# A gated pair of 2-D spectral filters: another layout for the narrow column's inverse and the scratch reads, merged constants, another order list

## The chip, the cores and the metric

The kernel runs on one core of a Trainium2 chip. The metric is the device time of one execution in microseconds (us); lower is better. Five engines work side by side, each on its own in-order queue: TensorE (PE; its weight loads are shown as PEld), VectorE (DVE), ScalarE (ACT), GpSimd (POOL) and SyncE (SP). Here SyncE issues nearly all DMA transfers, and sixteen DMA engines carry them.

## The reference

Two spectral filters, A and B, act on the same input `x` (1 x 2048 x 1024, bf16), and a gate per row mixes their results. `B_x` is not used.

```python
def filt(x, w_r, w_i):                          # w: 2048 x 513
    X = jnp.fft.rfft2(x.astype(jnp.float32), axes=(-2, -1))
    return jnp.fft.irfft2(X * (w_r + 1j * w_i), s=(2048, 1024),
                          axes=(-2, -1)).astype(jnp.bfloat16)

x = A_x
g = sigmoid((x * gate_w).sum(-1, keepdims=True))
out = g * filt(x, A_w_r, A_w_i) + (1 - g) * filt(x, B_w_r, B_w_i)
```

## The kernel before

All transforms are matmuls with constant matrices. The 2048 rows are split as `s = 16 * s2 + s1`, with `s2` on the 128 partitions and `s1` along the free dimension. The 1024 columns are folded by symmetry into sums and differences, so that the frequencies fall into an odd half (`par` 1) and an even half (`par` 0), each 256 wide. The frequency 512 of the column transform is left over: it is the "narrow column", handled by small steps of its own.

**Forward.** `ld x` loads the rows in nine transfers; `fold` (L228, VectorE) makes sums and differences; `f1` (L236, or `f1u`, L243, which does without a fold) transforms over `s2`; `ye` copies PSUM to the tile `y`. Then come eight units `u` (0 to 3 odd, 4 to 7 even). For each: `f2` (column transform, constant FD), `te` (copy), `f3` (over `s1`, constant WF), `xe` (copy), `prod` (VectorE, products with both filters' weights from a buffer `W`; two of the four buffers lie inside the tile `r`), `i1` (inverse over the 16 row frequencies, constant WI, in two halves), `re` (copy into one of three slots `rl`), and `wr` (L336), which writes the slot to a scratch tensor `scr` in DRAM, in 1 KB pieces.

**Scratch and inverse.** `rd` (L340) reads the scratch back with another meaning of the partitions: each of the 128 partitions gets `n` x 2 KB in one piece for `n` values of `s1`. `rd` of the odd half needs units 0 to 3 in scratch, `rd` of the even half units 4 to 7. It lands in the tile `r`, half `par`. For each pair of `s1` values, `v` from 0 to 7, `i2` (L371) multiplies by the gate's weighted matrices EA and EB, `ve` copies, `i3` or `i3u` (L387, L395, constant IG) does the column inverse, `ce`, `se` or `ue` copy, `pm` or `pmp` make sums and differences, `fin` joins the odd and the even half, and `st` (L434) stores. The odd half's inverse runs first; the even half's follows once `rd 0` has landed.

**Narrow column.** `l1`, `l2` (forward), `lp` (products, L297), `l3` (inverse, six matmuls, L301), `l3e` (copy to `zl`). Then `lx` (L311): a scatter of `zl` to the DRAM scratch `scn` in pieces of 4 bytes, and a load of it into `NL` with the other meaning of the partitions. `lf` (L315) copies parts of `NL` into the even half of `r`, over columns that `rd 0` has brought in, before `i2` reads them.

**Gate.** `gws` and `gh` (L344) transform the gate's weights, `zse` (L351) copies the result to `zs` and at once issues the load of `zt` from it; `gz` (L355), `sig`, and `gw` (L363), which makes EA and EB from the sigmoid `g` and the constant E.

**Order.** One list, `ORDER`, written out by hand at the end of the file, gives every step in turn. Each engine, SyncE too, takes its steps in the order of the list, and dependencies between tiles become semaphore waits. A letter says which engine does a copy or an elementwise step (`a` ScalarE, `d` VectorE, `p` GpSimd). So a transfer on SyncE that waits for its data holds back all transfers behind it. Eight semaphores are shared by the DMA transfers in turn, so that a transfer also waits for the one eight places ahead of it. All copies go through one helper (L196), all matmuls into eight PSUM banks `ps`.

Of the kernel before, what the change touches and what calls it, by code (L numbers as in the profile page):

```python
# [35 lines left out]
def make_constants():  # L36
# [8 lines left out]
    for q in range(64):  # L45
# [10 lines left out]
        E[2 * q], E[2 * q + 1] = ec, es  # L56
# [8 lines left out]
    c["F1"] = _bf16np(np.concatenate([F, -F, F], axis=1))  # L65
    c["EZ"] = _bf16np(EZ.reshape(128, 128) / 128)
    c["E"] = _bf16np(E)
    al = al.reshape(NT, 4 * 32, 32)
    c["WF"] = _bf16np(np.stack([-al.imag, al.real, al.imag], axis=2).transpose(1, 0, 2, 3))
# [9 lines left out]
    c["WI"] = _bf16np(np.tile(z.transpose(2, 0, 1, 3), (4, 1, 1, 1)))  # L79
    z = np.stack([np.concatenate([be.imag, -be.imag], axis=1), np.concatenate([be.real, be.real], axis=1)], axis=1)  # L80
    c["WN"] = _bf16np(np.tile(z.transpose(2, 0, 1, 3), (2, 1, 1, 1)))
# [17 lines left out]
    FN = -np.cos(np.pi * i)  # L99
    c["FD"] = _bf16np(FD.reshape(2, 128, 2, 2, 256).transpose(1, 2, 3, 0, 4))  # L100
    c["FN"] = _bf16np(FN.reshape(2, 128).T)
# [7 lines left out]
def gated_mix(ctx, tc, x_in, w_in, wn_in, gw_in, out, order):  # L109
# [18 lines left out]
    F1 = sb("f1", [3, 128])  # L128
    gws = sb("gws", [8])
    nc.scalar.dma_start(F1[:], dr["F1"].rearrange("p (a b) -> p a b", a=3))  # L130
    nc.scalar.dma_start(gws[:], gw_in)
# [7 lines left out]
    scn = dp.tile([2 * NT, 64, 2], BF16, name="scn")  # L139
    y = sb("y", [2, 2, 2, 64, NS1, 2])  # L140
    FD = sb("fd", [2, 2, 2, 256])
    FN = sb("fn", [2])
    nc.scalar.dma_start(FN[:], dr["FN"])
    WF = sb("wf", [NT, 3, 32])
    WI = sb("wi", [2, 3, 64])
    WN = sb("wn", [2, 2, 32])
    EZ = sb("ez", [128])
# [11 lines left out]
    wl = sb("wl", [2, 2 * NT, 2])  # L159
    pl = sb("pl", [2, 2 * NT, 2])  # L160
    zl = sb("zl", [2 * NT, 2])
    NL = sb("nl", [NS1, 2])
# [40 lines left out]
    def ld(what, *a):  # L203
        if what == "x":
            s0, n = a
            nc.sync.dma_start(x[:, s0:s0 + n, :], xv[:, s0:s0 + n, :])
        elif what == "w":
            u, s = a
            nc.sync.dma_start(flat(W[s]), w_in[u])
        elif what == "wl":  # L210
            nc.sync.dma_start(wl[:], wn_in.rearrange("p (t s a) -> p t s a", t=2, a=2))
        elif what == "wf":
            nc.sync.dma_start(WF[:, a[0]:a[1]], dr["WF"][:, a[0]:a[1]])
        else:
            t_ = {"FD": FD, "WI": WI, "WN": WN, "EZ": EZ, "E": E, "IG": IG}[what]
            nc.sync.dma_start(t_[:], dr[what])

    def gws_(eng):

        nc.vector.tensor_scalar(gh[:], gws[:], 0.25, None, ALU.mult)  # L220
# [76 lines left out]
    def lp(eng):  # L297
        xb = xl[:].rearrange("p (t s a) -> p t s a", t=1, a=1).to_broadcast([P, 2, 2 * NT, 2])
        nc.vector.tensor_tensor(pl[:], xb, wl[:], ALU.mult)

    def l3(g0):  # L301
        v = pl[:].rearrange("p t s a -> p t (s a)")
        for i, (o, lo, hi) in enumerate(((0, 2, 64), (64, 0, 64), (0, 0, 2))):
            for k in range(2):
                nc.tensor.matmul(PS[o // 2:o // 2 + 32, g0, lo:hi], lhsT=WN[o:o + 64, int(i == 2), k, :], rhs=v[o:o + 64, k, lo:hi],
                                 start=(k == 0), stop=(k == 1))

    def l3e(g0, eng):
        copy(eng, zl[0:64].rearrange("p s a -> p (s a)"), PS[0:64, g0, 0:64])

    def lx():  # L311
        nc.sync.dma_start(scn[:].rearrange("s p a -> p s a"), zl[0:64])
        nc.sync.dma_start(NL[:], scn[:].rearrange("s (j x) a -> (s j) x a", x=NS1))

    def lf(s0, n, eng):  # L315
        copy(eng, R[:, 0, s0:s0 + n, 512:1024:256], NL[:, s0:s0 + n, :])
# [23 lines left out]
    def rd(par, s0, n, t0=0, nt=NT):  # L340
        src = scr[par, 2 * t0:2 * t0 + 2 * nt].rearrange("t (j s r) c -> (t j) s (r c)", s=NS1, r=2)
        nc.sync.dma_start(R[8 * t0:8 * t0 + 8 * nt, par, s0:s0 + n, :], src[:, s0:s0 + n, :])
# [8 lines left out]
    def zse(g0, eng="a"):  # L351
        copy(eng, zs[:].rearrange("p q c s -> p (q c s)"), PS[:, g0, :])
        nc.sync.dma_start(zt[:], zs[0:97:32].rearrange("p q c s -> p (q c s)"))

    def gate_z(h, g0):  # L355
        for s in range(8):
            nc.tensor.matmul(PS[:, g0 + s // 4, (s % 4) * 128:(s % 4) * 128 + 128],
                             lhsT=zt[:, 8 * h + s:8 * h + s + 1].to_broadcast([P, 128]), rhs=EZ[:], start=True, stop=True)

# [74 lines left out]
    def st(v, s0=0, n=2):  # L434
# [3 lines left out]
               l3e=l3e, lx=lx, lf=lf, prod=prod, i1=i1, re=re, wr=wr, rd=rd, gws=gws_, gh=gate_hat, zse=zse, gz=gate_z, sig=sig,  # L438
# [73 lines left out]
def pack_w(mats):  # L512
# [4 lines left out]
    for q in range(64):  # L517
        rows = np.concatenate([(kk + 128 * k1) % S for kk in pair_k2(q)])
        v = a[rows].reshape(32, 2, 2, -1)
        for r in range(2):  # L520
            for z in range(2):
                wn[q % 2, r, :, z, q // 2] = v[:, :, (r + z) % 2, 512]
# [44 lines left out]
```

## Time and profile before

| | us |
|---|---|
| median of 3 runs | 129.66 (128.72 to 133.2) |
| profiled execution | 128.86 |
| its span, first to last instruction | 127.0 |

| engine | busy us | share of the span |
|---|---|---|
| VectorE | 98.5 | 77% |
| TensorE matmul | 97.9 | 77% |
| ScalarE | 87.9 | 69% |
| TensorE weight load | 71.6 | 56% |
| GpSimd | 2.6 | 2% |

The profile is of one execution. "Granted clock" is the TensorE clock in parts of full speed; it was 0.938 over the span. The sixteen DMA engines moved 36.34 MB. The page's slices show the span in 40 parts of 3.2 us; the digits are tenths of the time in which the DMA engines were busy, and the line below gives what they moved:

```profile
DMA  3999999991003999899999999999712999409884
GB/s 99 287 362 419 430 410 397 424 400 44 0 5 129 254 427 378 285 341 331 341 379 396 374 295 377 391 356 357 85 13 32 417 428 415 175 31 351 312 323 172
```

The page's issue rows give, for each kind of transfer, its size and the median time from issue to landing:

```profile
r<-scr SPq DMA_DIRECT2D x7, 1024.0 KB, 7.4
w<-in_w_dram SPq DMA_DIRECT2D x6, 1024.0 KB, 10.5
scr<-rl SPq DMA_DIRECT2D x12, 512.0 KB, 6.2
...
out_dram<-p SPq DMA_DIRECT2D x4, 512.0 KB, 2.6
```

Elsewhere a row such as `101.58 0.29 PE L378 MATMUL ... [5.94 <-DMA r<-scr]` has the start in us from the span's start, the length, the engine, the line of the kernel and its operation with output and input; the bracket has the idle time ahead of it and what ended it.

### The profile page before, as it was taken

To read this page: it belongs to the slowest core of one execution; us is meant where nothing else is said; L and a number is where in the kernel's file an instruction comes from. 1 tells how busy PE (TensorE), PEld (TensorE's weight loads), DVE (VectorE), ACT (ScalarE), POOL (GpSimd) and SP (SyncE) were. 2 spreads that over 40 slices of the span, in tenths; PEclk is the share of its full clock that TensorE was granted. 3 is DMA by queue.
4 is the path that set the end of the run, shared out by engine and by line. 5 is a ranking of instruction groups with operands and counts; after the bars stand their busy time and mean duration, and the time that the engine had idled before them with its cause. 6 is when DMAs were issued, how large, how long until landed. Compare 5 with 4: busy or idle time off the path is not lost. (4 is left out here: it accounts for less than half of the span.)

```text
span 127.0 us, 3857 instructions
## 1 busy us (share of the span) xinstructions
PE 97.9 (77%) x1695; PEld 71.6 (56%) x1696; DVE 98.5 (77%) x135; ACT 87.9 (69%) x86; POOL 2.6 (2%) x6
## 2 busy tenths in 40 slices
PE   6849998279897797969695998699991099999900
PEld 2538787156664465447344545278990099998300
DVE  0259898295999999998999577996892048999970
ACT  3139873187999999995986499976660058999630
POOL 1000000000000000000000420000000000000000
PEclk9999999958999999999999589999998559999996
DMA  3999999991003999899999999999712999409884
GB/s 99 287 362 419 430 410 397 424 400 44 0 5 129 254 427 378 285 341 331 341 379 396 374 295 377 391 356 357 85 13 32 417 428 415 175 31 351 312 323 172
DMA packets 17828, 36.34 MB, mean 286 GB/s; under 512 B 3988, under 2 KB 12436, under 8 KB 15892
## 3 DMA queue, kind: packets, MB, share of 16 engines
q1 hardware_dynamic: 17380, 36.00, 78.4%
q8 instruction: 13, 0.21, 0.6%
q10 hardware_dynamic: 432, 0.10, 0.4%
q14 instruction: 3, 0.02, 0.0%
HBM read 23.51 MB, written 12.59 MB: 284 GB/s over the span
## 5 line engine op out<-in xcount | busy, mean ns | idle before, releaser
L320 DVE TENSOR_TENSOR p<-x,w 128x2048 bf16<-128x2048 bf16 (+1 forms) x22 | 28.0, 1315 | 1.5 <-DMA w<-in_w_dram 0.9
L196 ACT CAST rl<-ps 128x1536 bf16<-128x1536 f32 (+2 forms) x16 | 23.2, 1470 | 2.6 <-PE ps L330 2.3
L330 PE MATMUL ps<-p,wi 32*64 32x512 bf16 x512 | 20.0, 409 | 4.3 <-ACT rl L196 1.2
L378 PE MATMUL ps<-g,r 128*128 128x128 bf16 x128 | 16.8, 229 | 5.9 <-DMA r<-scr 5.9
L378 PEld LDWEIGHTS <-r 128*128 128x128 bf16 x256 | 16.3, 103 | 6.8 <-DMA r<-scr 6.1
L196 ACT CAST y<-ps 128x1024 bf16<-128x1024 f32 (+1 forms) x17 | 14.2, 904 | 8.0 <-PE ps L240 7.3
L240 PE MATMUL ps<-f,r 128*128 128x256 bf16 x124 | 15.9, 290 | 3.2 <-DVE r L230 1.8
L378 PE MATMUL ps<-e,r 128*128 128x128 bf16 x128 | 16.8, 229 | 0.0
L240 PEld LDWEIGHTS <-r 128*128 128x128 bf16 x124 | 12.7, 104 | 6.1 <-DVE r L230 2.5
L330 PEld LDWEIGHTS <-wi 32*64 32x64 bf16 x512 | 9.1, 110 | 12.1 <-issue 8.8
L196 ACT CAST x<-ps 128x1024 bf16<-128x1024 f32 (+2 forms) x8 | 11.6, 1446 | 6.0 <-PE ps L271 6.0
L259 PE MATMUL ps<-fd,y 128*128 128x256 bf16 x128 | 15.2, 273 | 0.1
L230 DVE TENSOR_TENSOR r<-r 128x1024 bf16<-128x1024 bf16 (+1 forms) x16 | 10.3, 670 | 6.4 <-DMA r<-in_x_dram 6.3
L196 ACT CAST w<-ps 128x1024 bf16<-128x1024 f32 (+1 forms) x15 | 12.9, 953 | 1.8 <-PE ps L378 1.6
L259 PEld LDWEIGHTS <-y 128*128 128x128 bf16 x128 | 12.0, 98 | 3.3 <-issue 1.1
L196 ACT CAST t<-ps 128x1536 bf16<-128x1536 f32 (+3 forms) x9 | 12.2, 1350 | 1.9 <-PE ps L259 1.7
L196 DVE CAST rl<-ps 128x512 bf16<-128x512 f32 (+1 forms) x11 | 9.6, 879 | 2.3 <-ACT g L361 1.4
L271 PE MATMUL ps<-t,wf 32*32 32x256 bf16 (+1 forms) x384 | 6.5, 308 | 6.1 <-DMA wf<-cst_wf 2.3
L428 DVE TENSOR_TENSOR p<-p,y 128x1024 bf16<-128x1024 bf16 x16 | 10.2, 685 | 0.2
L271 PEld LDWEIGHTS <-wf 32*32 32x32 bf16 x384 | 4.6, 88 | 9.7 <-issue 6.2
L320 DVE TENSOR_TENSOR p<-x,r 128x2048 bf16<-128x2048 bf16 (+1 forms) x6 | 9.3, 1572 | 0.0
L196 DVE CAST w<-ps 128x512 bf16<-128x512 f32 x3 | 2.1, 689 | 7.5 <-PE ps L378 7.2
(55 smaller groups left out, 97.5 us busy)
## 6 DMA issues: line engine op xcount, KB each, us to landing
r<-scr SPq DMA_DIRECT2D x7, 1024.0 KB, 7.4
w<-in_w_dram SPq DMA_DIRECT2D x6, 1024.0 KB, 10.5
scr<-rl SPq DMA_DIRECT2D x12, 512.0 KB, 6.2
r<-in_x_dram SPq DMA_DIRECT2D x7, 512.0 KB, 7.8
r<-in_w_dram SPq DMA_DIRECT2D x2, 1024.0 KB, 11.2
scr<-rl SPq DMA_DIRECT2D x2, 1024.0 KB, 9.1
out_dram<-p SPq DMA_DIRECT2D x4, 512.0 KB, 2.6
out_dram<-p SPq DMA_DIRECT2D x8, 256.0 KB, 2.3
```

Of the source, the lines that this page charges most:

```text
L196: (nc.scalar.copy if eng == "a" else nc.vector.tensor_copy)(out=out, in_=in_)
L230: e.tensor_tensor(xf[uv][:, s0:s0 + n, :], x[:, s0:s0 + n, 0:512], x[:, s0:s0 + n, 512:1024], (ALU.add, ALU.subtract)[uv])
L240: nc.tensor.matmul(PS[:, g0 + k, blk * 256:blk * 256 + 256], lhsT=xf[uv][:, s0 + k, h * 256 + blk * 128:h * 256 + blk * 128 + 128], rhs=fn ...
L259: nc.tensor.matmul(PS[:, g0 + b, 256 * cs:256 * cs + 256], lhsT=y[:, par, blk, KK[par, cs], 4 * t:4 * t + 4].rearrange("p q s c -> p (q s ...
L271: nc.tensor.matmul(PS[qo:qo + 32, g0 + b, dst:dst + ln], lhsT=WF[32 * a:32 * a + 32, t, w, :], rhs=T[0][32 * a:32 * a + 32, b, src:src + l ...
L320: nc.vector.tensor_tensor(pr[u % 2][r][:, b0:b0 + nb], xb, W[s][:, b0:b0 + nb], ALU.mult)
L330: nc.tensor.matmul(PS[o:o + 64, g0 + 2 * (b % 2) + a // 2, :], lhsT=WI[q:q + 32, int(t == 0 and a == 0), ws, :], rhs=rhs, start=(k == 0), ...
L378: nc.tensor.matmul(PS[:, g0 + s, 128 * c:128 * c + 128], lhsT=R[:, par, s1, o:o + 128], rhs=Ew[:, s1, :], start=(ab == 0), stop=(ab == 1))
L428: e.tensor_tensor(OT[v % 4][:, :, k].rearrange("p s e m -> p e s m"), a, b, (ALU.add, ALU.subtract)[k])
```

## The change

Four things change.

The narrow column's inverse. `l3` now takes the products as the stationary operand and the constant WN as the moving one, so that the result leaves TensorE with row pairs on partitions, as `i2` wants them. It has 24 small matmuls instead of six; `l3e` copies straight to `NL`; `lx`, the scratch `scn` and the tile `zl` are gone. The products tile `pl` doubles to 256 elements per partition.

The partitions. For this the 128 partitions of the second half are ordered as (4, 32) and no longer as (32, 4): the constant E is reordered on the host, and `rd` reads `scr` with another pattern. Its source was 128 pieces at one stride; now it is 4 groups of 32 pieces, carried in the instruction as 4, then 32, then 4096 (or 2048) contiguous elements. The destination is the same 128 partitions of `r`.

The loads. F1 and FN come in one load (ScalarE's queue); the gate's weights come with `wl`; WF, WI, WN and EZ become one tile CW of 2176 columns with one load. `zt` is a step of its own (`ztd`), apart from `zse`.

The order list is new throughout. `f1u` is no longer used. `w 1` is loaded ahead of CW, and `w 0` behind it; IG goes behind `wr 0`, `wr 1` and `w 4`; E goes ahead of `wr 0`. `gh` and `zse` come after unit 1, and both halves of `gw` of the second half go to GpSimd. On SyncE the first `rd` stands ahead of `w 7`, and the last odd `rd` behind all `wr`.

```diff
-        E[2 * q], E[2 * q + 1] = ec, es
+        for cc, e in enumerate((ec, es)):
+            E[32 * (2 * (q % 2) + cc) + q // 2] = e
...
+    c["CW"] = np.concatenate([a.reshape(128, -1) for a in (WF, WI, WN, EZ)], axis=1)
...
     def lp(eng):
-        xb = xl[:].rearrange("p (t s a) -> p t s a", t=1, a=1).to_broadcast([P, 2, 2 * NT, 2])
-        nc.vector.tensor_tensor(pl[:], xb, wl[:], ALU.mult)
+        xb = xl[:].rearrange("p (k a t) -> p k a t", k=1, a=1).to_broadcast([P, 4, 2, 2 * NT])
+        nc.vector.tensor_tensor(pl[:], xb, wl, ALU.mult)
...
     def l3(g0):
-        v = pl[:].rearrange("p t s a -> p t (s a)")
-        for i, (o, lo, hi) in enumerate(((0, 2, 64), (64, 0, 64), (0, 0, 2))):
-            for k in range(2):
-                nc.tensor.matmul(PS[o // 2:o // 2 + 32, g0, lo:hi], lhsT=WN[o:o + 64, int(i == 2), k, :], rhs=v[o:o + 64, k, lo:hi],
-                                 start=(k == 0), stop=(k == 1))
+        for j in range(4):
+            o, cc = 64 * (j // 2), j % 2
+            for ab in range(2):
+                for k in range(4 if o == 0 else 2):
+                    nc.tensor.matmul(PS[32 * j:32 * j + 32, g0, 16 * ab:16 * ab + 16], lhsT=pl[o:o + 64, k, ab, :],
+                                     rhs=WN[o:o + 64, k // 2, k % 2, 16 * cc:16 * cc + 16], start=(k == 0), stop=(k == (3 if o == 0 else 1)))
 
     def l3e(g0, eng):
-        copy(eng, zl[0:64].rearrange("p s a -> p (s a)"), PS[0:64, g0, 0:64])
-
-    def lx():
-        nc.sync.dma_start(scn[:].rearrange("s p a -> p s a"), zl[0:64])
-        nc.sync.dma_start(NL[:], scn[:].rearrange("s (j x) a -> (s j) x a", x=NS1))
+        copy(eng, NL[:].rearrange("p a s -> p (a s)"), PS[:, g0, 0:32])
 
     def lf(s0, n, eng):
-        copy(eng, R[:, 0, s0:s0 + n, 512:1024:256], NL[:, s0:s0 + n, :])
+        copy(eng, R[:, 0, s0:s0 + n, 512:1024:256], NL[:, :, s0:s0 + n].rearrange("p a s -> p s a"))
...
-    def rd(par, s0, n, t0=0, nt=NT):
-        src = scr[par, 2 * t0:2 * t0 + 2 * nt].rearrange("t (j s r) c -> (t j) s (r c)", s=NS1, r=2)
-        nc.sync.dma_start(R[8 * t0:8 * t0 + 8 * nt, par, s0:s0 + n, :], src[:, s0:s0 + n, :])
+    def rd(par, s0, n):
+        src = scr[par].rearrange("t (j s) c -> j t (s c)", j=4)
+        nc.sync.dma_start(R[:, par, s0:s0 + n, :], src[:, :, 1024 * s0:1024 * (s0 + n)])
...
+    def ztd():
         nc.sync.dma_start(zt[:], zs[0:97:32].rearrange("p q c s -> p (q c s)"))
```

SyncE's transfers from the first `wr` to the last `rd`, in the order of each list (`wr u, s0, n`; `rd par, s0, n`):

```
before: wr 0 0 8 | E | w 4 | w 5 | wr 2 0 4 | EZ | wr 1 0 4 | wr 1 4 4 | wr 2 4 4 | wr 3 4 4 | wr 3 0 4 | w 6 |
        rd 1 4 4 | rd 1 0 4 | zt | rd 1 12 4 | w 7 | wr 4 0 8 | wr 5 4 4 | wr 5 0 4 | wr 6 0 4 | rd 1 8 4 |
        wr 6 4 4 | wr 7 0 4 | wr 7 4 4 | scn | NL | rd 0 2 2 | rd 0 0 2 | rd 0 4 4 | rd 0 8 4 | rd 0 12 4
after:  wr 0 0 8 | wr 1 4 4 | w 4 | IG | zt | w 5 | wr 2 0 8 | wr 1 0 4 | wr 3 0 4 | wr 3 4 4 | w 6 | wr 4 4 4 |
        rd 1 0 4 | w 7 | rd 1 4 4 | wr 4 0 4 | rd 1 8 4 | wr 5 0 4 | wr 5 4 4 | wr 6 0 8 | wr 7 4 4 | wr 7 0 4 |
        rd 1 12 4 | rd 0 0 2 | rd 0 2 2 | rd 0 4 4 | rd 0 12 4 | rd 0 8 4
```

More of the change, by code (lines that the diff above doesn't have):

```diff
@@ L64, in make_constants @@
     F = F.reshape(128, 128)
-    c["F1"] = _bf16np(np.concatenate([F, -F, F], axis=1))
-    c["EZ"] = _bf16np(EZ.reshape(128, 128) / 128)
+    FN = -np.cos(np.pi * np.arange(256)).reshape(2, 128).T
+    c["F1"] = _bf16np(np.concatenate([F, -F, F, FN], axis=1))
+    EZ = _bf16np(EZ.reshape(128, 128) / 128)
     c["E"] = _bf16np(E)
     al = al.reshape(NT, 4 * 32, 32)
-    c["WF"] = _bf16np(np.stack([-al.imag, al.real, al.imag], axis=2).transpose(1, 0, 2, 3))
+    WF = _bf16np(np.stack([-al.imag, al.real, al.imag], axis=2).transpose(1, 0, 2, 3))
     be = np.zeros((2, 2, 16, 2, NS1), dtype=complex)
@@ L78, in make_constants @@
     z = np.stack([z, -z, np.stack([-be.imag, be.real], axis=-1).reshape(2, 32, 64)], axis=1)
-    c["WI"] = _bf16np(np.tile(z.transpose(2, 0, 1, 3), (4, 1, 1, 1)))
+    WI = _bf16np(np.tile(z.transpose(2, 0, 1, 3), (4, 1, 1, 1)))
     z = np.stack([np.concatenate([be.imag, -be.imag], axis=1), np.concatenate([be.real, be.real], axis=1)], axis=1)
-    c["WN"] = _bf16np(np.tile(z.transpose(2, 0, 1, 3), (2, 1, 1, 1)))
+    WN = _bf16np(np.tile(z.transpose(2, 0, 1, 3), (2, 1, 1, 1)))
+    c["CW"] = np.concatenate([a.reshape(128, -1) for a in (WF, WI, WN, EZ)], axis=1)
     i = np.arange(256)
@@ L98, in make_constants @@
             IG[0, 1, 0] /= 2
-    FN = -np.cos(np.pi * i)
     c["FD"] = _bf16np(FD.reshape(2, 128, 2, 2, 256).transpose(1, 2, 3, 0, 4))
-    c["FN"] = _bf16np(FN.reshape(2, 128).T)
     IG = IG.reshape(2, 2, 2, 128, 256) / (S * D)
@@ L108, in gated_mix @@
 @with_exitstack
-def gated_mix(ctx, tc, x_in, w_in, wn_in, gw_in, out, order):
+def gated_mix(ctx, tc, x_in, w_in, wn_in, out, order):
     nc = tc.nc
@@ L127, in gated_mix @@
         nc.tensor.matmul(PS[:, 7, :], lhsT=warm[:, 0:128], rhs=warm[:], start=True, stop=True)
[L128 to L131, printed above, removed]
+    F1N = sb("f1", [386])
+    F1, FN = F1N[:, 0:384].rearrange("p (a b) -> p a b", a=3), F1N[:, 384:386]
+    nc.scalar.dma_start(F1N[:], dr["F1"])
     R = sb("r", [2, NS1, 1024])
@@ L138, in gated_mix @@
     scr = dp.tile([2, 2 * NT, P, 512], BF16, name="scr")
-    scn = dp.tile([2 * NT, 64, 2], BF16, name="scn")
     y = sb("y", [2, 2, 2, 64, NS1, 2])
     FD = sb("fd", [2, 2, 2, 256])
[L142 to L147, printed above, removed]
+    CW = sb("cw", [NT * 96 + 384 + 128 + 128])
+    WF = CW[:, 0:1536].rearrange("p (t w c) -> p t w c", t=NT, w=3)
+    WI = CW[:, 1536:1920].rearrange("p (k w c) -> p k w c", k=2, w=3)
+    WN = CW[:, 1920:2048].rearrange("p (k w c) -> p k w c", k=2, w=2)
+    EZ = CW[:, 2048:2176]
     E = sb("e", [NS1, 128])
@@ L158, in gated_mix @@
     xl = sb("xl", [2 * NT])
[L159 to L162, printed above, removed]
+    WL = sb("wl", [264])
+    wl, gws = WL[:, 0:256].rearrange("p (k a t) -> p k a t", k=4, a=2), WL[:, 256:264]
+    pl = sb("pl", [4, 2, 2 * NT])
+    NL = sb("nl", [2, NS1])
     gwz = sb("gwz", [8, 32])
@@ L210, in ld @@
         elif what == "wl":
-            nc.sync.dma_start(wl[:], wn_in.rearrange("p (t s a) -> p t s a", t=2, a=2))
-        elif what == "wf":
-            nc.sync.dma_start(WF[:, a[0]:a[1]], dr["WF"][:, a[0]:a[1]])
+            nc.sync.dma_start(WL[:], wn_in)
         else:
-            t_ = {"FD": FD, "WI": WI, "WN": WN, "EZ": EZ, "E": E, "IG": IG}[what]
+            t_ = {"FD": FD, "CW": CW, "E": E, "IG": IG}[what]
             nc.sync.dma_start(t_[:], dr[what])
     def gws_(eng):
-        nc.vector.tensor_scalar(gh[:], gws[:], 0.25, None, ALU.mult)
+        nc.vector.tensor_scalar(gh[:], gws, 0.25, None, ALU.mult)
         nc.vector.tensor_tensor(gq[:, 0].rearrange("p l b -> p (l b)"), gh[:, 0:4], gh[:, 4:8], ALU.add)
@@ L357, in gate_z @@
             nc.tensor.matmul(PS[:, g0 + s // 4, (s % 4) * 128:(s % 4) * 128 + 128],
-                             lhsT=zt[:, 8 * h + s:8 * h + s + 1].to_broadcast([P, 128]), rhs=EZ[:], start=True, stop=True)
+                             lhsT=zt[:, 8 * h + s:8 * h + s + 1].to_broadcast([P, 128]), rhs=EZ, start=True, stop=True)
     def sig(h, g0):
@@ L437, in gated_mix @@
     ops = dict(ld=ld, fold=fold, f1=f1, f1u=f1u, ye=ye, f2=f2, te=te, f3=f3, xe=xe, l1=l1, l1e=l1e, l2=l2, l2e=l2e, lp=lp, l3=l3,
-               l3e=l3e, lx=lx, lf=lf, prod=prod, i1=i1, re=re, wr=wr, rd=rd, gws=gws_, gh=gate_hat, zse=zse, gz=gate_z, sig=sig,
+               l3e=l3e, zt=ztd, lf=lf, prod=prod, i1=i1, re=re, wr=wr, rd=rd, gws=gws_, gh=gate_hat, zse=zse, gz=gate_z, sig=sig,
                gw=gate_w, i2=i2, ve=ve, i3=i3, i3u=i3u, ce=ce, se=se, ue=ue, pm=pm, pmp=pmp, fin=fin, finp=finp, st=st)
@@ L445 @@
 ORDER = [
[33 rows of a table removed]
-    ("prod", 7, 1, 0, 0, 2), ("gz", 1, 0), ("sig", 1, 0), ("prod", 7, 1, 1, 0, 2), ("prod", 7, 1, 0, 2, 2), ("i2", 1, 0, 2),
[25 rows of a table removed]
[56 rows of a table added]
 ]
@@ L514, in pack_w @@
     w = np.zeros((len(UNITS), P, 4, 4, 256), dtype=a.dtype)
-    wn = np.zeros((2, 2, 32, 2, 2 * NT, 2), dtype=a.dtype)
+    wn = np.zeros((2, 2, 32, 2, 2, 2, 2 * NT), dtype=a.dtype)
     k1 = np.arange(16)
@@ L521, in pack_w @@
             for z in range(2):
-                wn[q % 2, r, :, z, q // 2] = v[:, :, (r + z) % 2, 512]
+                wn[q % 2, r, :, int(q == 0), z, :, q // 2] = v[:, :, (r + z) % 2, 512]
         for par in range(2):
@@ L553 @@
     xp = _np.ascontiguousarray(_np.asarray(inputs["A_x"])[:, :, cols])
-    gw = _np.ascontiguousarray(_np.asarray(inputs["gate_w"])[cols].reshape(8, P).T)
+    wn = _np.concatenate([wn, _np.asarray(inputs["gate_w"])[cols].reshape(8, P).T], axis=1)
     arrays, args = {}, []
-    for name, a in (("x", xp), ("w", w), ("wn", wn), ("gw", gw)):
+    for name, a in (("x", xp), ("w", w), ("wn", wn)):
         arrays[f"in_{name}_dram"] = a
```

114 rows, old and new, of the table ORDER are left out of this document.

## The prediction

> **What bounds the kernel now.** I read the page's slices and DMA queues first, then the DMA issues, the SyncE queue in time, TensorE's waits, and a table of stretches from the last products on. That table: length, busy time of PE, PEld, DVE, ACT and POOL, TensorE's clock, DMA share, GB/s.
>
> ```profile
> 84.60:95.60 11.00, 11.00 (x152) 10.16 (x150) 9.21 (x16) 7.51 (x11) 0.00 (x0) 1.00 0.66 168
> 95.60:101.60 6.00, 0.06 (x2) 0.02 (x2) 0.73 (x2) 0.00 (x0) 0.00 (x0) 0.67 0.66 229
> 101.60:104.70 3.10, 3.10 (x32) 3.06 (x33) 1.19 (x2) 1.59 (x3) 0.00 (x0) 0.54 1.04 439
> 104.70:122.70 18.00, 15.94 (x179) 13.11 (x177) 17.30 (x39) 15.20 (x17) 0.00 (x0) 1.00 0.66 261
> ```
>
> Between 95.6 and 101.6 us nothing computes, and the next stretch runs at a granted clock of 0.54; from there to the end VectorE is the bound (17.30 of 18.00). TensorE has two long waits:
>
> ```profile
> 24.19 0.81 PE L271 MATMUL ps<-t,wf 32*32 32x512 bf16 x48 [2.32 <-DMA wf<-cst_wf]
> ...
> 101.58 0.29 PE L378 MATMUL ps<-g,r 128*128 128x128 bf16 x1 [5.94 <-DMA r<-scr]
> ```
>
> The second is a wait for the even half's reads (L342). SyncE's queue, in time, says why:
>
> ```profile
> 62.31 0.81 SPq L342 DMA_DIRECT2D r<-scr  x2
> ...
> 85.84 0.89 SPq L312 DMA_DIRECT2D scn<-zl  x1
> 96.19 0.33 SPq L313 DMA_DIRECT2D nl<-scn  x1
> 96.70 2.24 SPq L342 DMA_DIRECT2D r<-scr  x5
> ```
>
> L313 waits 9.4 us on the narrow column's scatter, and five reads stand behind it. But the last `wr`, issued at 85.39, landed only 10.1 us later, at 95.5, so only 1.2 us is SyncE's own wait. In the trace's packets that `wr` shares the engines with some 2,000 scatter packets of 4 bytes, and from 91 to 95 us they move 21 GB/s or less but for one microsecond at 36.
>
> One rate matters below, from the DMA view of 104 to 107 us, when only reads run:
>
> ```profile
> DMA packets 168, 1.26 MB, mean 421 GB/s; under 512 B 15, under 2 KB 15, under 8 KB 15
> ...
> q1 hardware_dynamic: 167, 1.25, 99.3%
> ```
>
> 421 GB/s on sixteen busy engines is 26 GB/s each. An 8,192-byte packet takes 309 ns (median and first percentile alike; none of 1,930 took under 307, however few were in flight), a 4,096-byte packet 159, a 1,024-byte packet of a `wr` 46. So the limit is the engine's, and a read on fewer engines is slower in proportion.
>
> **The change part by part.** *Reads of the scratch (the part that decides).* `rd` moves the same 8.39 MB in the same 8 or 4 KB pieces, but its source now counts 4, then 32, where it counted 128. One transfer of before has such a source: `zt`, 4 by 32. Its completion shows in the trace as one update of the semaphore at 67.70 us and four more at 69.46 to 69.86, where the other transfers leave sixteen; its 128 packets are never more than four in flight, while `nl`'s 128 packets, with 128 outermost, are up to ten. I read this as: `zt` ran on four engines, and every `rd` will.
>
> [...]
>
> On four engines a 1 MB read is 32 packets on each, 32 x 309 ns = 9.9 us, and a 512 KB read 32 x 159 ns = 5.1 us. If it is always the same four, they come one after another: 7 x 9.9 + 2 x 5.1 = 79.4 us. Other transfers, queued between, need the four as well: one `w` load, 8 x 309 ns = 2.5 us, and seven half units of `wr`, 32 x 46 ns = 1.5 us each, 10.3. Sum 92.2 us. Add 1 us from issue to first packet (96.70 to 97.7) and 1 us for the landing.
>
> *Where this chain starts.* The first read waits for units 0 to 3 to be in scratch and, on SyncE, behind half of unit 4's `wr`. Before it was issued at 62.31. VectorE's work from the first product to that half's copy is 13 half products x 1.22 + 4 whole x 2.28 + 2 copies x 1.22 + 10 x 0.69 = 34 us, less about 2 because neighbours overlap. The first product comes at about 25: `f3` without its 2.32 us (next part) at 21.9, then two copies and `xe`. 25 + 32 + some 3 for ScalarE's share and SyncE = 60. Bounds: 57 with nothing added, 64 if the old start holds and the extra half unit delays it.
>
> *Its end.* 60 + 92.2 + 2 = 154.2 us. The last two reads serve `lf 8 8`, and VectorE waits there. Before, the last read landed at 110.4 and the span ended at 127.0, so 16.6 us follow; VectorE has 13.4 us of rows after that `lf` now, 12.3 before: 17.7. Span 171.9; with the 1.86 us around it (128.86 less 127.0) about 173.8. I take 173.5. The profiled run stands 0.8 us under the median of three, 129.66.
>
> *No scatter and no `lx`.* Removes the 1.2 us of SyncE, at most 5.3 if the last `wr` would land at 91.4 without the 4-byte packets. TensorE's wait it shortens is then filled by reads that land later: nothing in my forecast, 5.3 if reads are as fast as before.
>
> *`l3` on 24 instead of 6 matmuls.* The six took 0.26 us: 18 x 0.043 = 0.8 more at most, 0.2 by `l2`'s rows (64 in 0.7 us). `lp` doubles its elements, 0.28 to about 0.42 us. Both stand ahead of `i2(1,6)`, which waits for a read: covered. Without that cover, 1 us. `l3e` and `lf` keep their size.
>
> *Merged constants.* WI, WF, WN and EZ are the same 544 KB in one load, ahead of `w 0` and behind one `w` fewer, and WF ended 2.32 us late. Worth 1 to 2.3 us at the start; I took 2.3. `w 0` now lands near 24, when the first product wants it. ScalarE issues one load, not three, 0.9 us it spent before its table load; its first copy waits for TensorE until 6.80 anyway. IG, 768 KB, moves into the busy middle (1.8 us at 421 GB/s), E leaves it for the idle stretch at 29 to 38 us (1.2).
>
> *First blocks.* They fold instead of `f1u`: 0.42 us more on VectorE, four matmuls fewer, in a stage where VectorE waited 6.3 us for `x`: nothing.
>
> *Order.* Row sums give VectorE 2.0 us less over the kernel, ScalarE 0.7 more, PE 0.4 less. GpSimd takes both `gw` of the second half, 2.12 us each, early before `i2(1,4)`. `zt` is fetched some units before use, so TensorE's 1.53 us wait for it goes. New waits: on SyncE `w 7` is behind the first read, so it lands near 75 (61 + 9.9 + 2.5 and the landing) and VectorE, ready for unit 7 at about 67 (57 and 10 us of rows), waits 8 us with the last copies of units 6 and 7 and their `wr` behind; on ScalarE `lf 0 4` stands ahead of `ve(1,6)` and holds it until the even reads land. In the forecast both lie inside the chain of reads, which has `rd(1,4)` and `rd(1,8)` queued to about 95 us.
>
> **The rivals.** *Reads keep sixteen engines (faster).* For: packets and bytes are unchanged, and `zt`'s four-count source lies in SBUF, not DRAM. Against: no other difference explains four updates. Then DMA sets the pace: 17.6 MB (all `wr`, the odd reads, four `w`, IG) from the first `wr`, at 39.2 less the 2.3 of WF, at the 350 GB/s of the stretches of 40 to 85 us (335 to 359) is 50.2 us: 87.1. One for landing, 4.9 from issue to `i2` (96.70 to 101.58): 93.0. From `i2` to the end took 25.5; 0.9 less at full clock. Span 117.6, time 119.5.
>
> *Four engines, but other four each time.* The reads then overlap. For: nothing records which engine carried a packet. Against: `zt` is a single case and can't tell. The last odd and the five even reads, queued from 88, need 5.1 + 9.9 us in two rounds plus 2: 105. Plus 17.7 and 1.9: 125.
>
> *The chain has holes.* If the four engines ever idle because `wr` for units 6 and 7 come late (VectorE's 8 us for `w 7`, then slots of `rl` that wait for landings), each microsecond adds one. I expect the last `wr` by 89 (75, 9 us of rows, then unit 4's slot, free at 86, and a copy) and the earlier queue lasts to 61 + 3 x 9.9 + 2.5 + 3 x 1.5 = 98, so 9 us of slack; 8 us of holes would give 182.
>
> **How the numbers follow.** Reads on the same four engines: 0.87, because the one transfer of that shape did so and the packet time leaves no spare speed; holes are 0.07 of that. Sixteen: 0.09. Other four: 0.04. Range: low end with the start 3 us earlier and the 12.8 us of other transfers half out of the way, less 1.7 of the tail, 162; high end with the start 4 later and 8 us of holes, 186. It leaves out the 0.13 of the rivals and some 0.06 of the first case. Two per cent of 129.66 is 2.6 us, about what a measurement can tell: faster is below 127.1, slower above 132.3. Sixteen engines are faster, other four mostly between 119 and 131, hence 0.11 faster, 0.02 the same, 0.87 slower.
>
> **What would show it.** Each 1 MB `r<-scr` row should take 10 us alone and 20 or more queued; DMA share near 0.25 and about 106 GB/s for most of 100 to 154 us; TensorE's wait `<-DMA r<-scr` tens of microseconds in several pieces; VectorE waiting for `w 7`; the last read landing near 154 and some 18 us after it. The wait for WF should be gone. It would be wrong if reads land in 7 us with share near 1.

## The result, and the profile after

The changed kernel takes 179.5 us (median of four runs, 177.57 to 182.23) against 130.91 us (128.72 to 133.2) of the kernel before in the same runs: a ratio of 1.379, with a 95% interval of 1.351 to 1.407. The ratio compares the faster executions of each kernel (178.66 and 177.57 us with 128.72 and 129.66), since some executions of either run some per cent longer. The forecast was 173.5 us, in a range of 162 to 186. The profiled execution is the longest of the four, 182.23 us; its span is 180.2 us, and the mean granted clock 0.808.

First the page's slices, now 4.5 us each. The two rows below are the DMA engines' busy tenths and what they moved:

```profile
DMA  5999992049999996222372782222222242213666
GB/s 183 309 407 421 417 415 110 4 157 320 406 367 340 291 256 178 85 98 105 123 266 105 275 275 105 109 104 109 104 109 105 105 193 105 109 76 120 233 234 234
```

Over the first sixteen slices the picture is much that of before. Then, until the last read lands at 161 us, the digit is mostly 2 and the rate mostly 104 to 109 GB/s: a quarter of the sixteen engines at work (a share of 0.27 from 111.5 to 161.2 us), and a quarter of the 421 GB/s that reads alone moved before. Where the digit is higher, `wr`, or at 144 us a store, run on the other engines. The issue row of the reads has no landing time any more:

```profile
r<-scr SPq DMA_DIRECT2D x7, 1024.0 KB
```

The page works a landing time out from sixteen completion updates, and each read now leaves five, one about at issue and four at the end (the first, issued at 60.39 us, at 61.37 and at 78.84 to 80.07), as `zt` did. The page's chain that ended last has become a chain of transfers:

```profile
DMA 46%; PE 21%; ACT 14%; SPq 10%; issue 4%; DVE 2%; DVEq 0%; ACTq 0%
```

and the waits (engine, line, what was waited for: us in total, times, longest) show who pays:

```profile
PEld L374 <- DMA r<-scr: 37.2, 6, 13.8
PE ps L374 <- DMA r<-scr: 35.5, 6, 13.5
ACT r L195 <- DMA r<-scr: 24.8, 2, 19.4
...
DVE r L195 <- DMA r<-scr: 16.8, 1, 16.8
...
DVE p L314 <- DMA w<-in_w_dram: 14.1, 2, 11.8
```

L374 is `i2`. Its one wait for reads (5.94 us before) is now several, and they come in the rhythm of the chain: the TensorE rows that follow begin right after the landings of reads at 103.58, 121.49 and 141.42 us.

```profile
103.63 0.29 PE L374 MATMUL ps<-g,r 128*128 128x128 bf16 x1 [6.67 <-DMA r<-scr]
121.53 0.29 PE L374 MATMUL ps<-g,r 128*128 128x128 bf16 x1 [8.67 <-DMA r<-scr]
...
141.47 0.23 PE L374 MATMUL ps<-g,r 128*128 128x128 bf16 x1 [4.70 <-DMA r<-scr]
```

The table of stretches (length, busy time of PE, PEld, DVE, ACT, POOL, then granted clock, DMA share, GB/s) shows the first read's stretches, the last five reads after the odd half was in, and the tail behind the last landing:

```profile
60.40:69.20 8.80, 6.29 (x169) 3.06 (x166) 6.48 (x7) 6.87 (x6) 0.00 (x0) 0.86 0.99 275
69.20:80.00 10.80, 5.65 (x94) 2.61 (x90) 1.54 (x1) 5.43 (x5) 4.23 (x2) 0.50 0.33 105
111.50:161.20 49.70, 16.40 (x168) 14.56 (x166) 10.22 (x17) 8.87 (x12) 0.00 (x0) 0.70 0.27 114
161.20:175.80 14.60, 12.73 (x111) 10.28 (x112) 13.14 (x29) 9.64 (x10) 0.00 (x0) 0.85 0.48 183
```

In the 49.7 us of the third row no engine is busy for more than 16.4 us. SyncE's queue, at last, holds a line that the prediction had not expected:

```profile
60.39 0.56 SPq L336 DMA_DIRECT2D r<-scr  x1
62.16 0.34 SPq L208 DMA_DIRECT2D w<-in_w_dram  x1
62.55 0.54 SPq L336 DMA_DIRECT2D r<-scr  x1
...
64.18 15.19 SPq L336 DMA_DIRECT2D r<-scr  x1
```

The third read's issue takes 15.19 us. It ends at 79.37, while the first read lands at 80.07 and the next two 12.4 and 11.2 us after one another.

The transfers queued between the reads show in the trace's updates which engines they wait for. Of the sixteen updates of `w 7`, issued at 62.16 behind the first read, twelve had come by 71.49 us; the other four came at 81.01 to 82.44, right after that read's last update at 80.07. The `wr` issued at 63.77 left twelve by 72.22 and four at 92.25 to 93.64, right after the second read's at 92.43. So each read holds four of the sixteen engines, by these updates the same ones, in the order of the queue, and what stands behind it has its last four updates late (9.5 and 20.0 us after the twelfth).

### The profile page after: what moved, and what is told of

Its sections match the earlier page's. It is cut to its first block, busy times and chain, and to the rows that moved or that the text cites. A ratio compares the mean times of both kernels' runs of the same rounds, so it can differ in the third digit from the quotient of the medians.

```text
span 180.2 us, 3868 instructions
## 1 busy us (share of the span) xinstructions
PE 109.3 (61%) x1709; PEld 79.9 (44%) x1710; DVE 96.9 (54%) x131; ACT 88.5 (49%) x85; POOL 4.7 (3%) x7
## 4 chain that ended last, share of the span: by engine, by line
DMA 46%; PE 21%; ACT 14%; SPq 10%; issue 4%; DVE 2%; DVEq 0%; ACTq 0%
DMA r<-scr 21%; DMA scr<-rl 21%; SPq L336 6%; PE ps L237 6%; PE ps L256 5%; ACT rl L195 4%; DMA r<-in_x_dram 4%; ACT t L195 4%; PE ps L374 3%; SPq L332 3%; ACT x L195 3%; PE ps L388 2%; PE ps L397 2%; ACT y L195 2%; PE ps L268 1%
## 5 line engine op out<-in xcount | busy, mean ns | idle before, releaser
L374 PE MATMUL ps<-g,r 128*128 128x128 bf16 x128 | 25.1, 289 | 51.0 <-DMA r<-scr 35.5
L374 PEld LDWEIGHTS <-r 128*128 128x128 bf16 x256 | 24.0, 137 | 53.8 <-DMA r<-scr 37.2
L314 DVE TENSOR_TENSOR p<-x,w 128x2048 bf16<-128x2048 bf16 (+1 forms) x20 | 28.0, 1432 | 14.1 <-DMA w<-in_w_dram 14.1
L374 PE MATMUL ps<-e,r 128*128 128x128 bf16 x128 | 25.1, 289 | 0.0
L324 PE MATMUL ps<-p,cw 32*64 32x512 bf16 x512 | 20.9, 434 | 3.4 <-ACT x L195 1.3
L237 PEld LDWEIGHTS <-r 128*128 128x128 bf16 x128 | 12.4, 99 | 7.2 <-DVE r L227 4.3
L195 ACT CAST x<-ps 128x2048 bf16<-128x2048 f32 (+2 forms) x8 | 13.7, 1714 | 1.4 <-PE ps L268 1.2
L324 PEld LDWEIGHTS <-cw 32*64 32x64 bf16 x512 | 9.1, 115 | 11.9 <-issue 9.0
L195 DVE CAST v<-ps 128x1024 bf16<-128x1024 f32 (+1 forms) x3 | 3.1, 1044 | 16.8 <-PE ps L374 16.8
L195 ACT CAST t<-ps 128x1536 bf16<-128x1536 f32 (+2 forms) x9 | 10.5, 1165 | 3.0 <-PE ps L268 1.5
L195 ACT CAST v<-ps 128x1024 bf16<-128x1024 f32 (+1 forms) x6 | 5.6, 941 | 12.4 <-PE ps L374 12.4
L195 DVE CAST cs<-ps 128x512 bf16<-128x512 f32 (+1 forms) x4 | 3.8, 956 | 13.3 <-PE ps L388 9.7
```

The costliest lines, as they stand in the source:

```text
L195: (nc.scalar.copy if eng == "a" else nc.vector.tensor_copy)(out=out, in_=in_)
L237: nc.tensor.matmul(PS[:, g0 + k, blk * 256:blk * 256 + 256], lhsT=xf[uv][:, s0 + k, h * 256 + blk * 128:h * 256 + blk * 128 + 128], rhs=fn ...
L314: nc.vector.tensor_tensor(pr[u % 2][r][:, b0:b0 + nb], xb, W[s][:, b0:b0 + nb], ALU.mult)
L324: nc.tensor.matmul(PS[o:o + 64, g0 + 2 * (b % 2) + a // 2, :], lhsT=WI[q:q + 32, int(t == 0 and a == 0), ws, :], rhs=rhs, start=(k == 0), ...
L374: nc.tensor.matmul(PS[:, g0 + s, 128 * c:128 * c + 128], lhsT=R[:, par, s1, o:o + 128], rhs=Ew[:, s1, :], start=(ab == 0), stop=(ab == 1))
```

## The experiments

**What is to be told apart.** My theory: the read's pattern (4, 32, ...) gives it to four DMA engines, always the same, and their chain sets the time. Rivals: something else in the new list or the layout costs the time; and, inside the theory, the wait for `w 7` or the lost cover of the scatter.

**The pattern undone, in the changed kernel.** Each read is issued as four transfers of 32 partitions, so that each source counts 32:

```diff
-        nc.sync.dma_start(R[:, par, s0:s0 + n, :], src[:, :, 1024 * s0:1024 * (s0 + n)])
+        for j in range(4):
+            nc.sync.dma_start(R[32 * j:32 * j + 32, par, s0:s0 + n, :], src[j, :, 1024 * s0:1024 * (s0 + n)])
```

> The changed kernel with one edit: each read of the scratch is issued as four transfers of 32 partitions, so that 32 stands first in each source instead of 4. Same bytes, pieces, addresses, partitions and order. Theory (a transfer runs on as many of the sixteen engines as its outermost count allows): the reads spread over all engines again, a 1 MB read lands in some 7 us, the chain of 92 us is gone, and the time falls from 179 us to the 119.5 of the forecast's rival, up to 124 because SyncE issues 27 more transfers at about 0.4 us. Rival 1 (the new order of partitions, pieces 64 KB apart where they were 16 KB apart, makes the reads slow): stays near 179. Rival 2 (the new order list is what costs): stays above 140.

136.17 us (131.33 to 137.37, four runs; before, beside it, 130.64). Most of the loss is gone, but the runs lie 7 to 13 us above the 124 us that I had allowed. Its page shows a second effect:

```profile
DMA  4999999920089999999999999999999997047385
GB/s 120 337 369 422 419 413 421 413 94 5 0 271 321 392 381 354 341 280 326 253 256 203 308 274 350 344 351 227 228 245 225 225 230 216 30 155 285 120 311 213
```

In the seven slices from the 28th on, nine tenths of all engines are busy, and they move 216 to 245 GB/s, half of 421. The reads do run on sixteen engines (sixteen updates each), but the trace's packets of 8 KB take 612 ns at the median there (92 to 112 us), not 309. So the number of engines is not all.

**The pattern alone, in the kernel before.** Its scratch gets a gap of one row after each sixteenth, eighth or fourth, so that the read's source counts 16, 8 or 4 outermost; order list, partitions and narrow column stay. (Writes that cross a gap are cut in two or more; with four groups none does.)

```diff
-    scr = dp.tile([2, 2 * NT, P, 512], BF16, name="scr")
+    G, T_ = 16, 2          # 8, 4 and 4, 8 in the other two
+    scr = dp.tile([2, G, T_ * P + 1, 512], BF16, name="scr")
...
+        src = scr[par, :, 0:T_ * P, :].rearrange("g (q s r) c -> g q s (r c)", s=NS1, r=2)
+        nc.sync.dma_start(R[:, par, s0:s0 + n, :], src[:, :, s0:s0 + n, :].rearrange("g q s c -> g q (s c)"))
```

> The kernel before, with a gap of 1 KB after each sixteenth of a half of the scratch, so that the source of each read counts 16, then 8, where it counted 128. Order of partitions, pieces and order list are those of before; writes go in pieces of two, 18 transfers more. Theory: sixteen stands first, so all sixteen engines work, and the time is that of before (about 130 us), at most 4 us more for SyncE's issues. Rival 1 (a source pattern of three dimensions is slow in itself): far above, 170 or more, as in the changed kernel.

> As the kernel with gaps after each sixteenth, but after each eighth: the sources count 8, then 16. Theory: eight engines, 5 us for 1 MB. From the first read at 62.3 us: 6 of queue, 4 odd reads of 5 and 14.5 us of writes and weights give 103, the scatter 2 to 3, even reads 20, the tail 16.6: a span near 142, time 140 to 146. Rival 1 (three dimensions slow in themselves): the same time as with sixteen groups, whatever that is.

> As above with gaps after each quarter: the sources count 4, then 32, as in the changed kernel, but in the kernel before's order of partitions and list. Theory: four engines, 10 us for 1 MB: 62.3 + 6 + 40 + 14.5 + 2.5 + 40 + 16.6 = 182, time 178 to 188, so that the pattern alone makes the whole loss. Rival 2 (the order list or the order of partitions costs): below 150.

| groups | updates at a read's end | time, us | 8 KB packets while reads run, median | GB/s then |
|---|---|---|---|---|
| none (before) | 16 | 130.64 | 309 ns | 421 |
| 16 | 16 | 147.43 (145.3 to 148.07) | 606 ns (112 to 128 us) | 222 |
| 8 | 8 | 178.56 (one run) | 619 ns (130 to 160 us) | 111 to 123, with a store 176 |
| 4 | 4 | 196.87 (one run) | 311 ns (140 to 180 us) | 89 to 106, with a store 188 |

The last row carries the theory: the pattern alone, without one other part of the change, costs as much as the change and more. It lies 9 us above the range that I gave; in the old list the gate's `zt` also stands behind slow reads, and TensorE waits 23.6 us for it, which the sum left out. The number of updates follows the outermost count in each case. The engines' busy share goes with it: 1.01 with 16 groups (113 to 125 us), 0.53 with 8 (133 to 158 us, a store among the reads), and mostly the digit 2 in the page's slices with 4 (140 to 175 us).

The rows for 16 and 8 are misses, by 17 and by more than 30 us: the ratio of the first to before is 1.125 (1.106 to 1.144), where I had expected none. The DMA view of the 16-group kernel from 113 to 125 us, when it reads, shows busy engines at half the rate:

```profile
DMA packets 356, 2.66 MB, mean 222 GB/s; under 512 B 32, under 2 KB 32, under 8 KB 32
...
q1 hardware_dynamic: 355, 2.65, 100.9%
```

So there is a second factor: the same packet takes 309 ns or 600, by the pattern.

**Which side makes a packet slow.** The two candidates are the strided source in DRAM and the partitions that are written. The weights' loads have a contiguous source, so I cut those, in the kernel before, into four transfers of 32 partitions:

```diff
-            nc.sync.dma_start(flat(W[s]), w_in[u])
+            for j in range(4):
+                nc.sync.dma_start(flat(W[s])[32 * j:32 * j + 32], w_in[u, 32 * j:32 * j + 32])
```

> The kernel before with each 1 MB load of the weights, whose source is one contiguous block, issued as four transfers of 32 partitions each. It tells apart why the reads split by 32 partitions ran at half the rate on all sixteen engines. If the engines are slow because they then write into neighbouring partitions (the destination side), the weight packets of 8 KB take about 600 ns instead of about 310, a weight load lands 4 to 5 us later than its like before, and the kernel takes 135 to 150 us. If the cause is the strided source in DRAM, the weight packets stay at about 310 ns and the time within 3% of that before.

140.83 us (one run), and packets of 604 ns (median of those that start from 16 to 62 us, where weights are loaded; before, 312 in the same stretch). The source is contiguous, so its stride is not needed for the effect.

Then eight transfers of 16 partitions, from the same contiguous rows, once into 16 partitions in a row and once into every eighth:

```diff
+            for j in range(8):
+                nc.sync.dma_start(flat(W[s])[16 * j:16 * j + 16], w_in[u, 16 * j:16 * j + 16])      # in a row
+                nc.sync.dma_start(flat(W[s])[j:128:8], w_in[u, 16 * j:16 * j + 16])                 # every eighth
```

> The kernel before with each 1 MB load of the weights issued as eight transfers of 16 partitions in a row; all of them still run on sixteen engines. Split into 32 partitions in a row the 8 KB packets took 550 to 640 ns instead of 309. If engines share paths into the memory by the partitions that they write, and 32 partitions in a row reach half as many paths as engines, then 16 in a row reach a quarter: packets of about 1.2 us, and weights that move at about 105 GB/s. If a transfer cut into pieces is slow by itself, whatever it writes, the packets stay near 600 ns.

> The same eight transfers of 16 partitions for each weight load, from the same contiguous source, but each writes every eighth partition instead of 16 in a row (the rows of the weights are stored in that order). [...] If cutting the transfer decides, both kernels show the same packets.

149.13 and 147.33 us (one run each). From 16 to 68 us the packets take 711 ns at the median in a row (633 to 881 between the quartiles) and 509 every eighth (373 to 578). The transfers are alike but for the partitions, so these matter: if cutting alone decided, both kernels would show the same packets. In a row the size is not the one expected (1.2 us), and idle engines don't explain it: while sixteen of these transfers of 128 KB were issued, over 12.65 us, the engines' busy share was 1.05 and everything together moved 232 GB/s. Every eighth, it was 0.87 and 256 GB/s over 12.44 us. Several of these transfers, to different partitions, were in flight at once; whether that is why the factor stays small wasn't tried. The shared paths that I supposed stay a guess of mine: no run here shows one. Nor are 32 partitions in a row slow everywhere: the four-group read writes them so, and its packets took 311 ns. That the partitions written matter is shown, why they do is not.

**The wait for the last weights.** In the changed kernel, `w 7` is issued ahead of the first read:

```diff
-    ("rd", 1, 0, 4), ("prod", 6, 0, 0, 0, 4), ("ld", "w", 7, 1), ...
+    ("prod", 6, 0, 0, 0, 4), ("ld", "w", 7, 1), ("rd", 1, 0, 4), ...
```

> The changed kernel with the last weight load issued ahead of the first read instead of behind it. If the chain of reads on four engines sets the time, VectorE's wait of 11.8 us for these weights vanishes and the time stays where it is, within 2% of the changed kernel (177 to 182 us), since the reads begin no earlier and end as late. If that wait is part of the loss, the time falls by as much as 11.8 us, to 166 to 172 us.

179.48 us (177.67 and 181.29), as the chain of reads demands. (In the profiled execution, the shorter one, the last read lands at 156.38 us, 4.8 before that of the changed kernel, whose own runs differ by 4.7.) The wait is gone; the group of the products, which had 14.1 us idle ahead of it in the changed kernel, has none:

```profile
L314 DVE TENSOR_TENSOR p<-x,w 128x2048 bf16<-128x2048 bf16 (+1 forms) x20 | 30.0, 1534 | 0.0
```

A wait of 11.8 us on VectorE was worth nothing, because reads landed too late anyway.

**The scatter.** The prediction priced its place at 1.2 to 5.3 us. In the kernel before I moved the products, the matmuls and the scatter early, and left only the load of `NL` behind the last `wr`:

```diff
-    ... ("l2e", 4, "a"), ("sig", 0, 6),
+    ... ("l2e", 4, "a"), ("sig", 0, 6), ("lp", "d"), ("l3", 4), ("l3e", 4, "a"), ("lx",),
...
+    ... ("wr", 7, 4, 4), ("ln",),
```

> The kernel before with the narrow column's scatter moved ahead: its products, its matmuls and the scatter stand right after the first sigmoid, some 20 us earlier, and only the load of the result stays behind the last write. All the work is the same. If the scatter's place on the queue between the last writes and the second half's reads cost time, the time falls by 1.2 to 5.3 us (0.9% to 4%). If other transfers cover it, or the bound lies in TensorE there, it stays within 1%.

134.78 us, a ratio of 1.038 (1.029 to 1.046): slower. The place was badly chosen. SyncE came to the scatter at 71.82 us, and `w 7` stood behind it: issued at 72.55 instead of 67.84, it made VectorE wait 6.3 us. So once more, with the scatter behind the writes of unit 5:

> The kernel before with the narrow column's products and matmuls early, as in the run that moved the scatter early, but with the scatter placed behind the writes of unit 5, so that the last weight load and those writes are not queued behind it. In that run the scatter's wait held the last weight load for 4.7 us, and VectorE waited 6.3 us for it; if this made it slower, this one is back at 128 to 131 us or below. If the scatter's old place between the last writes and the second half's reads cost 1.2 to 5.3 us, it is that much below 130; if it was covered, within 1% of the kernel before.

131.97 us against 131.68, a ratio of 1.022 (0.989 to 1.055): no gain to be seen. SyncE's queue shows that the scatter then holds the writes, and through them the reads:

```profile
73.88 0.68 SPq L312 DMA_DIRECT2D scn<-zl  x1
...
89.61 1.47 SPq L315 DMA_DIRECT2D nl<-scn  x1
97.25 2.32 SPq L344 DMA_DIRECT2D r<-scr  x5
```

The five even reads start at 97.25; before it was 96.70. While the scatter's packets of 4 bytes are under way little else moves (two slices of this run have 55 and 41 GB/s): issued at 73.88, it lands at 87.95, and the `wr` issued right behind it at 74.61 lands at 89.62. So at this place it cost about as much as at the old one.

**A kernel that beats both.** If only the pattern is wrong, the rest can be kept. This kernel is the changed one with the old order of partitions, hence the old read, and a narrow column that still leaves TensorE on those partitions: the stationary operand has 128 columns in the order (t, j), with zeros for the other `j`. It lies in the tile `T`, free by then, and GpSimd clears it.

```diff
-        src = scr[par].rearrange("t (j s) c -> j t (s c)", j=4)
-        nc.sync.dma_start(R[:, par, s0:s0 + n, :], src[:, :, 1024 * s0:1024 * (s0 + n)])
+        src = scr[par].rearrange("t (j s r) c -> (t j) s (r c)", s=NS1, r=2)
+        nc.sync.dma_start(R[:, par, s0:s0 + n, :], src[:, s0:s0 + n, :])
...
+        for j in range(4):
+            o = slice(64 * (j // 2), 64 * (j // 2) + 64)
+            nc.vector.tensor_tensor(pl[o, j % 2, :, :, :, j], xb[o], wl[o], ALU.mult)
...
+        for ab in range(2):
+            for cc in range(2):
+                for k in range(4):
+                    nc.tensor.matmul(PS[:, g0, 16 * ab:16 * ab + 16], lhsT=pl[:, cc, k, ab].rearrange("p t j -> p (t j)"),
+                                     rhs=WN[:, k // 2, k % 2, 16 * cc:16 * cc + 16], start=(cc == 0 and k == 0), stop=(cc == 1 and k == 3))
```

> The changed kernel with its order list, its merged constants and its narrow column without scratch, but with the scratch of the columns read back uniformly onto 128 partitions as in the kernel before (partition = 4 t + j). So that the narrow column still needs no second trip through memory, its inverse leaves TensorE on those partitions: 16 matmuls with a stationary operand of 128 columns of which half are zeros, built by four VectorE operations on 64 partitions and one GpSimd memset. If the read's four DMA engines are the whole loss and the order list is sound, this gives the changed kernel's row sum with reads that land on time: 117 to 124 us, every read with 16 completion updates and about 310 ns for each 8 KB packet, no wait of TensorE for a read above 4 us. If something else in the new list or in the removed scratch costs time as well, it stays above the time before, 129 to 133 us or more.

122.67 us (122.23 to 123.05, four runs), a ratio to before of 0.945 (0.938 to 0.953). Its page, slices of 3.0 us, and the row of the reads, again with a landing time:

```profile
DMA  3999999992006999999899999590999993445884
GB/s 79 368 339 412 421 415 422 422 406 103 5 0 237 310 380 405 364 356 330 306 390 416 377 402 386 182 333 16 325 371 407 427 430 136 180 174 225 325 325 174
...
r<-scr SPq DMA_DIRECT2D x7, 1024.0 KB, 10.4
```

The longest wait of TensorE's matmuls there is 6.4 us for a copy, and none is for a read. So the rest of the change, taken together and with this narrow column, loses nothing and gains 7 us: the reads' pattern is the whole loss. A part that costs a little may still hide in the gain.

**Which part brings that gain.** The same kernel with the old order list, less the steps that fell away:

> The kernel that beat both (uniform reads, narrow column without scratch, merged constants), with its order list put back to that of the kernel before, less the two scratch transfers of the narrow column and the loads that were merged. Its profiled execution took 122.7 us against about 130 of the kernel before. If the new list brings this gain, the old list gives 127 to 131 us. If the merged constants and the scratch that fell away bring it, the old list gives 121 to 125 us.

124.72 us (123.05 to 128.12, four runs) beside 129.97 of before: some 5.3 of the 7.4 us come without the new list. (The 122.7 us that this expectation names is the median of the kernel that beat both; its profiled execution took 122.23.) SyncE, freed of the scatter, issues the five even reads at 92.01 us:

```profile
83.52 5.46 SPq L335 DMA_DIRECT2D scr<-rl  x3
92.01 2.25 SPq L339 DMA_DIRECT2D r<-scr  x5
```

That is 4.7 us earlier than 96.70, and the profiled execution is 4.7 us shorter (124.18 against 128.86). Merging the constants brought nothing here: the wait for WF is still there, now for CW.

```profile
23.66 0.81 PE L267 MATMUL ps<-t,cw 32*32 32x512 bf16 x48 [2.55 <-DMA cw<-cst_cw]
```

The other 2 us go with the new list, and this wait is the nearest row for them. The spreads of the two kernels touch (123.05), so this last share isn't shown. That the 4.7 us are the scatter's rests on one profiled execution of each kernel.

## Why the prediction was right, point by point

**The mechanism** held: four engines, always the same, in a chain, forecast at 0.87. The updates, the quarter share, the 105 GB/s, the cure by another pattern and the loss from the pattern alone all show it. The rivals fall: sixteen engines and "other four each time" by the split updates of `w 7` and the `wr`, and by the 10 us from landing to landing (121.49, then 126.43 and 131.44 for the two half-size reads, 141.42, 151.31, 161.19), holes in the chain by the same numbers: the last five reads follow each other without a gap, and the stretch before them takes no longer than its sum.

**The sum of the chain** was forecast as 92.2 us of engine time. From the first read's landing (80.07) to the last (161.19) it took 81.1; the sum less that first read's 9.9 is 82.3. The 1 us for the landing was taken without a row; the last packet ended at 160.65 us, 0.5 before the last update.

**The mis-sized term** is where the chain starts. I put the first read's issue at 60 and it came at 60.39, but I let it land at 60 + 1 + 9.9 + 1 = 71.9, and it landed at 80.07, 8.2 us later. The sum had assumed four engines that stand free and packets of 309 ns. In the trace, `w 6` and half of unit 4's `wr` were issued ahead of the read, and their last updates came at 65.62 and 66.82; and from 63 to 72 us, while reads, `w 7` and `wr` ran together, the 8 KB packets took 573 ns at the median. From 72 to 82 us it is 314. The run with `w 7` ahead of the first read tells the two apart in part: there the 8 KB packets of 63 to 72 us took 309 ns at the median, and the read landed 10.4 us after the last update of the transfers ahead of it (67.28 and 77.71), against 13.3 us here (66.82 and 80.07). As far as these last updates show it, some 3 of the 8.2 us go with the slow packets beside `w 7`, and most of the rest with the queue ahead of the read. With 1.2 us gained later, the last read lands at 161.19 instead of 154.2, 7.0 us late. "None of 1,930 took under 307" was right, but a floor is not the duration: the experiments above show the same packet at 600.

**The tail** took 19.0 us from the last landing to the end, forecast 17.7, at a granted clock of 0.85 over most of it (before, 1.00 from 104.7 to 122.7). The 7.0, these 1.3 and the 0.2 by which the time around the span grew (2.03 against 1.86) are the difference of the profiled execution to the forecast, 182.23 against 173.8. The median of the runs lies 2.7 us lower. That the time stayed inside the range owes something to the range's width: 8 us of its high end stood for holes in the chain, which didn't come, and covered a late start, for which it had 4.

**The wait for `w 7`**: forecast 8 us, measured 11.8; it grew with the first read's delay, since `w 7` stands behind it: the wait ended at 82.53 us, with the last of its four late updates (82.44). That it is hidden was right, as its removal showed.

**Constants.** The wait for WF is gone in the changed kernel, as forecast; the row has no bracket, and no wait of TensorE for `zt` is left either:

```profile
22.60 0.81 PE L268 MATMUL ps<-t,cw 32*32 32x512 bf16 x48
```

But I gave two reasons, one load instead of several and one `w` fewer ahead of it. With the old list the merged load waits as long as before, so it is the place in the list.

**No scatter** was forecast as worth nothing in the changed kernel, which no run there tests, and bounded at 5.3 us were reads fast. With fast reads and the old list it shows 4.7: near the upper end. I had read only the 1.2 us as SyncE's own, and the rest as a `wr` made late by small packets; the run with the scatter behind the writes of unit 5 agrees, since no time was gained there.

**The rival of sixteen engines** had a price, 119.5 us. The kernel that has them and the new list took 122.67 (with a narrow column of its own), 3 us more. The sum left out waits such as TensorE's 6.4 us for a copy; what the 3 us are made of wasn't taken apart.

**Not tested alone:** the 24 matmuls of `l3`, the folds of the first blocks, and `lf 0 4` ahead of `ve(1,6)`. The last shows as ScalarE's wait of 19.4 us in the changed kernel, inside the chain.

## What to carry to other kernels

Look at the outermost dimension of a DMA's pattern when a layout changes: bytes, piece size and issue count can all stay, and the transfer still loses engines (four late updates instead of sixteen here, and 104 to 109 GB/s instead of 421), which the number of completion updates shows at once. Keep 128 partitions at one stride on both sides where that is possible (421 GB/s here, 222 with 16 groups); a narrow result can be brought to them by zeros in a matmul's operand, which cost little here (122.67 us for the kernel that has them), while cutting the wide transfer to suit it cost far more (179.5 us, and 136.17 with the reads cut by 32 partitions). And a wait that is long in the profile (11.8 us here) may be worth nothing as long as another chain ends later.

## What the runs showed of the hardware that I had not expected

- Sixteen busy engines can move half: 216 to 245 GB/s with reads cut by 32 partitions, about 222 with 16 groups of eight partitions, where uniform reads moved 421. The 8 KB packet then took 612 and 606 ns instead of 309, and 604 with a contiguous source too.
- Reads of the eight-group pattern (16 partitions in a row to a group) left eight updates, those of the four-group pattern (32 in a row) four. Eight were no faster than four: a 1 MB read landed every 9.2 us (140.89, 150.13, 159.25), against 9.9 us. The eight took 619 ns for a packet, the four 311.
- A DMA's issue can hold SyncE: 15.19 us for the third read in the changed kernel, 10.28 us for `w 7` in the four-group kernel, where issues of the kernel before took 0.3 to 1.6. Both stood behind reads on four engines. Whether a full queue of those engines holds them wasn't tried.
- The scatter of 8 KB in 4-byte pieces took 10.3 us from issue to landing, and neither of the two places tried for it saved time.
- In the wait for reads TensorE's granted clock was 0.50 to 0.70, and 0.85 over most of the work that followed.
